# Weight sums rebuilt inside SBUF: a copy of the high parts and an accumulating transfer of the low parts, instead of a round trip through device memory

## Chip, cores and metric

The kernel runs on one core of one Trainium2 chip. The metric is the device time of one execution in microseconds (us). Before the change it is 1271.15 us, the median of three runs (1270.35 to 1272.01). The engines are named as in the profile: PE (TensorE, matrix products), DVE (VectorE), ACT (ScalarE), POOL (GpSimd), SP (SyncE, which here only issues transfers).

## The reference

Two stages, all in float32. First a channel attention on q, k, v of shape 2 x 6016 x 256; then a SwiGLU block on the 12032 rows of its output, with weights of 256 x 1536, 256 x 1536 and 1536 x 256.

```python
qn = q / (norm(q, axis=1) + 1e-6);  kn = k / (norm(k, axis=1) + 1e-6)
s  = kn.transpose(0, 2, 1) @ qn / tau          # 256 x 256 for each batch
a  = softmax(s, axis=-1)
x  = (v @ a).reshape(12032, 256)
xn = x / sqrt(mean(x*x) + 1e-6) * rms_g
g, val = xn @ w_gate, xn @ w_val               # 12032 x 1536 each
out = (g * sigmoid(g) * val) @ w_out           # 12032 x 256
```

## The kernel before

Every float32 product of the second stage is made of three matmuls on rounded operands: a value is kept as a high part (rounded to the type fp32r) and a low part (the rest, rounded), and high x high, high x low and low x high are added. So each weight stands twice in SBUF: `w_hl[0]` holds the high parts, `w_hl[1]` the low parts, for 12 chunks f = 0 to 11 of 128 hidden channels each.

The rows of x go in blocks j of 3 or 4 tiles of 128 rows. A step (j, f) is chunk f of block j. Blocks 0 and 1 are computed plainly (`emit_hidden`: six matmuls for `pg`, six for `pv`, ACT makes the silu, DVE multiplies into `zh` and splits the result into gx, gy or gz by turns; two steps later the PE matmuls `po` use it). From block 2 on a step uses seven products instead of eight (`new_products`), and for these the kernel needs sums and differences of weight columns: `build_s` makes them for the pairs p = 0 to 5 of chunks (2p, 2p + 1).

The weights come in as 64-bit words. In the steps of block 0 they are loaded (`load_w`), decoded on DVE and ACT into a float32 tile `wx` (`decode_w`, lines 119 to 138; two such tiles take turns) and split (`split_w`, line 144). Beside them the loads `raw` of q and k of the second batch run, whose scores PE computes in the same steps.

`build_s(p, piece)` works in four pieces, which stand in the steps of blocks 0 and 1 as a table of steps counted from (1, 0) has it:

```python
at_step = [
    (-2, 0, 3, 4), (-1, 2, 5, 6), (4, 5, 6, 7), (6, 8, 9, 10), (7, 9, 10, 11), (10, 12, 13, 14),
]
```

Piece 0 fills a tile `t` (called `wk` in the profile) of 128 x 1024 floats, 512 KB, with the float32 weights of two chunks; piece 1 is four DVE operations on it (line 621); piece 2 rounds on ACT (line 624); piece 3 takes the rests on DVE (line 627: two into `s`, one into `w`). There are two buffers: even p use one, odd p the other, so piece 0 of pair p waits for piece 3 of pair p - 2. The table gives pair 2 one step between pieces 0 and 1; pairs 3, 4 and 5 have two.

Each engine does its instructions in the order in which they are written. SP issues transfers one after another too: an issue that waits holds all that follow. In SP's queue of block 1 stand the 16 small transfers of `emit_xT_move` (line 553), which bring a transposed block `xw` into place as `xnT`; block 2 needs them.

POOL, in blocks 0 and 1, does the small operations behind the row norms (`ss` at line 484, `rr` at line 488, which ACT waits for to write `xn` at line 500), the low parts `vt` of v (line 417), and for block 2 the differences `xp` (lines 574 and 579) and the low parts `xt` (line 593). It also issues the transfers of line 145.

Of the kernel before, what the change touches and what calls it, by code (L numbers as in the profile page):

```python
# [8 lines left out]
F32 = mybir.dt.float32  # L9
# [3 lines left out]
ALU = mybir.AluOpType  # L13
AX = mybir.AxisListType

P = 128
# [3 lines left out]
def kernel(  # L20
# [17 lines left out]
    nc = tc.nc  # L38
# [3 lines left out]
    KC = C // P  # L42
    NF = DFF // P
# [35 lines left out]
    w_hl = [const.tile([P, NF * WF + 8 * (1 - i)], F32R, name=f"w{i}") for i in range(2)]  # L79
    w_hl = [  # L80
        w[:, 4 * (1 - i):4 * (1 - i) + NF * WF].rearrange("p (f n) -> p f n", f=NF)
        for i, w in enumerate(w_hl)
    ]
# [5 lines left out]
    def f32(ap):  # L89
        return ap.bitcast(F32)  # L90
# [8 lines left out]
    wval = {}  # L99
# [38 lines left out]
            )  # L138
            wval[f] = x.bitcast(F32)

    dram = ctx.enter_context(tc.tile_pool(name="dram", bufs=1, space=bass.MemoryType.DRAM))
    kept = [dram.tile([P, KC * 2 * P], F32, name=f"kept_{f}") for f in range(NF)]

    def split_w(f, engine=nc.gpsimd):
        nc.gpsimd.dma_start(out=kept[f], in_=wval[f][:, :KC * 2 * P])
        nc.scalar.activation(out=w_hl[0][:, f, :], in_=wval[f], func=AF.Copy)
        engine.tensor_tensor(
            out=w_hl[1][:, f, :], in0=wval.pop(f), in1=f32(w_hl[0][:, f, :]), op=ALU.subtract,
        )
# [6 lines left out]
    for b, sizes in enumerate(([2] * 2 + [4] * 9 + [2] * 3 + [1], [CH] * 11 + [3])):  # L156
        t = 0
# [174 lines left out]
    t = 0  # L332
# [268 lines left out]
    def build_s(p, piece):  # L601
        f0, f1 = 2 * p, 2 * p + 1
        if piece == 0:
            tag = "so1" if p % 2 else "wk"
            s_tmp[p] = pool[tag].tile([P, 4, 2 * P], F32, tag=tag, name=f"wk_{p}")

        t = s_tmp[p]
        if piece > 1:
            hi, lo = ([x[:, p, :2], x[:, p, 2], w[:, f1, :2 * P]] for x, w in zip(s_hl, w_hl))
            src = (t[:, 2:4], t[:, 0], t[:, 1])  # L610
        if piece == 0:
            for i, f in enumerate((f0, f1)):
                nc.sync.dma_start(
                    out=t[:, 2 * i:2 * i + 2].rearrange("p i n -> p (i n)"), in_=kept[f]
                )
        elif piece == 1:
            for o, i0, i1, op in (
                (3, 2, 3, ALU.add), (2, 0, 2, ALU.subtract),
                (0, 3, 0, ALU.subtract), (1, 1, 0, ALU.subtract),
            ):  # L620
                nc.vector.tensor_tensor(out=t[:, o], in0=t[:, i0], in1=t[:, i1], op=op)  # L621
        elif piece == 2:
            for o, x in zip(hi, src):
                nc.scalar.activation(out=o, in_=x, func=AF.Copy)
        else:
            for o, x, y in zip(lo, src, hi):
                nc.vector.tensor_tensor(out=o, in0=x, in1=f32(y), op=ALU.subtract)
# [371 lines left out]
    with tc.manual_schedule():  # L999
# [30 lines left out]
        def stir(n, name):  # L1030
# [11 lines left out]
            4: lambda: load_w(0),  # L1042
            7: lambda: (load_w(1), decode_w(0)),
            8: lambda: split_w(0),
            10: lambda: load_v_rows(0),
            11: lambda: decode_w(1),
            12: lambda: split_w(1),
            13: lambda: load_w(2),
        }
        for i in range(nch):  # L1050
            n = chunks[0][i][1]
# [93 lines left out]
        for f in range(NF):  # L1145
            go = [lambda: None]
            if f + 3 < NF:
                go = [lambda f=f: decode_w(f + 3, 0), lambda f=f: decode_w(f + 3, 1)]
            if f + 2 < NF:
                go.append(lambda f=f: split_w(f + 2, nc.vector))  # L1150
            if f + 3 < NF:
                go.append(lambda f=f: decode_w(f + 3, 2))
            weights[0, f] = go
            n = 2 if f % 2 else 1

            def more(n=n):
                fill(n)
                for _ in range(n):
                    square()
                    add()  # L1160

            at(0, f, more)
            if f + 5 < NF:
                at(0, f, lambda f=f: load_w(f + 5))
# [30 lines left out]
        for i in (2, 3, 0, 1):  # L1195
            for p in range(NP):
                j, f = divmod(NF + at_step[p][i], NF)
                go = lambda p=p, i=i: build_s(p, i)
                if j == 1:
                    weights.setdefault((j, f), [lambda: None]).append(go)  # L1200
                else:
                    at(j, f, go)
# [238 lines left out]
```

## Time and profile before

| What | Value |
|---|---|
| Three runs | 1270.35, 1271.15, 1272.01 us |
| The profiled execution | 1274.14 us, of which its span is 1272.4 us |
| PE busy | 1250.7 us (98%) |
| DVE, ACT, POOL busy | 875.0, 868.5, 793.6 us (69%, 68%, 62%) |
| Mean granted clock of PE | 0.997 of full speed |
| Transfers on POOL's queue (12 of 256 KB, line 145) | 3.15 MB |

The span begins with the first instruction. Blocks 0 and 1 lie between about 73 and 200 us; from about 206 us on the steps of seven products repeat to the end. A matmul's busy time says little by itself, since matmuls are pipelined; where PE loses time is seen in what it waits for. DVE's share is a mean over stages: in blocks 0 and 1 it has the decoding of the weights and the pieces of `build_s` to do beside the steps.

### The profile page before, as it was taken

To read this page: it belongs to the slowest core of one execution; us is meant where nothing else is said; L and a number is where in the kernel's file an instruction comes from. 1 tells how busy PE (TensorE), PEld (TensorE's weight loads), DVE (VectorE), ACT (ScalarE), POOL (GpSimd) and SP (SyncE) were. 2 spreads that over 40 slices of the span, in tenths; PEclk is the share of its full clock that TensorE was granted. 3 is DMA by queue.
4 is the path that set the end of the run, shared out by engine and by line. 5 is a ranking of instruction groups with operands and counts; after the bars stand their busy time and mean duration, and the time that the engine had idled before them with its cause. 6 is when DMAs were issued, how large, how long until landed. Compare 5 with 4: busy or idle time off the path is not lost.

```text
span 1272.4 us, 25236 instructions
## 1 busy us (share of the span) xinstructions
PE 1250.7 (98%) x9245; PEld 1196.4 (94%) x9245; DVE 875.0 (69%) x1571; ACT 868.5 (68%) x1771; POOL 793.6 (62%) x637
## 2 busy tenths in 40 slices
PE   9998989999999999999999999999999999999998
PEld 8798989999999999999999999999999999999997
DVE  5788867558767657667767667767766766766764
ACT  5566647677776786776677677667677777777653
POOL 0221224575777777777677777777777777776742
PEclk9999989999999999999999999999999999999999
DMA  8979332020220220220220211211211211211110
GB/s 296 318 247 303 114 82 65 17 35 18 51 34 18 51 34 18 51 34 18 45 41 18 45 27 32 43 26 34 41 27 34 40 26 37 37 23 27 18 18 17
DMA packets 231004, 78.20 MB, mean 61 GB/s; under 512 B 191200, under 2 KB 220128, under 8 KB 230880
## 3 DMA queue, kind: packets, MB, share of 16 engines
q1 hardware_dynamic: 229024, 72.13, 24.0%
q0 software_dynamic: 960, 3.15, 0.6%
q8 instruction: 72, 1.18, 0.4%
q10 hardware_dynamic: 896, 1.31, 0.4%
q14 instruction: 52, 0.43, 0.1%
HBM read 49.55 MB, written 15.47 MB: 51 GB/s over the span
## 4 chain that ended last, share of the span: by engine, by line
PE 84%; DVE 5%; DMA 5%; issue 2%; ACT 2%; SPq 1%; POOL 1%; POOLq 0%; DVEq 0%; ACTq 0%
PE pu L764 43%; PE po L940 26%; PE pq L764 7%; PE px L459 5%; PE s L185 2%; DMA raw<-in_k_dram 2%; PE po L890 1%; DVE wk L621 1%; SPq L553 1%; DMA raw<-in_q_dram 1%; DVE acc L210 1%; DMA wraw<-in_moe_w_out_dram 1%; DMA wraw<-in_moe_w_gate_dram 0%; DMA kept<-wx 0%; ACT xn L475 0%
## 5 line engine op out<-in xcount | busy, mean ns | idle before, releaser
L764 PE MATMUL pu<-xt,w 128*128 128x256 f32 x2376 | 407.8, 280 | 0.5 <-DVE zv L793 0.3
L764 PE MATMUL pu<-xt,s 128*128 128x256 f32 x2376 | 367.8, 281 | 0.9 <-ACT t L800 0.8
L764 PEld LDWEIGHTS pu<-xt,w 128*128 128x128 f32 x2376 | 344.0, 188 | 14.0 <-DVE zg L793 1.0
L764 PEld LDWEIGHTS pu<-xt,s 128*128 128x128 f32 x2376 | 327.3, 188 | 14.0 <-ACT zg L827 1.2
L732 POOL TENSOR_TENSOR gy<-zg,gy 128x512 fp32r<-128x512 f32 x131 | 182.3, 1392 | 150.3 <-ACT gy L726 86.3
L732 POOL TENSOR_TENSOR gx<-zg,gx 128x512 fp32r<-128x512 f32 (+1 forms) x131 | 201.1, 1535 | 86.5 <-ACT gx L726 84.9
L805 ACT ACTIVATE t<-pu 128x512 f32<-128x512 f32 x264 | 158.2, 599 | 98.6 <-PE pu L764 80.6
L940 PE MATMUL po<-gx,w 128*128 128x256 f32 (+1 forms) x927 | 197.1, 330 | 0.0
L793 DVE TENSOR_TENSOR zv<-pu,t 128x512 f32<-128x512 f32 x132 | 90.6, 686 | 112.9 <-ACT zg L827 83.3
L812 DVE TENSOR_TENSOR zg<-zg,zv 128x768 f32<-128x768 f32 x132 | 154.0, 1167 | 14.4 <-ACT t L800 0.5
L800 ACT ACTIVATE t<-pu 128x256 f32<-128x256 f32 x264 | 100.7, 381 | 86.7 <-PE pu L764 85.1
L726 ACT ACTIVATE gx<-zg 128x512 fp32r<-128x512 f32 (+1 forms) x132 | 95.8, 726 | 74.7 <-DVE zg L821 35.5
L940 PEld LDWEIGHTS po<-gx,w 128*128 128x128 f32 x927 | 136.5, 188 | 6.3 <-ACT os L976 0.2
L718 DVE TENSOR_TENSOR zg<-zg 128x256 f32<-128x256 f32 x228 | 97.0, 425 | 65.6 <-POOL gx L732 59.8
L764 PE MATMUL pq<-xt,w 128*128 128x256 f32 x792 | 135.9, 280 | 0.0
L793 DVE TENSOR_TENSOR zg<-pu,t 128x512 f32<-128x512 f32 x132 | 89.9, 681 | 48.5 <-PE pu L764 27.3
L940 PE MATMUL po<-gy,w 128*128 128x512 f32 x414 | 118.1, 393 | 0.0
L821 DVE TENSOR_TENSOR zg<-pu,zg 128x256 f32<-128x256 f32 x132 | 55.9, 424 | 87.6 <-PE pu L764 85.9
L732 POOL TENSOR_TENSOR gz<-zg,gz 128x512 fp32r<-128x512 f32 x57 | 113.4, 1989 | 0.0
L764 PEld LDWEIGHTS pq<-xt,w 128*128 128x128 f32 x792 | 112.0, 189 | 0.0
L809 ACT ACTIVATE zg<-zg 128x768 f32<-128x768 f32 x132 | 110.4, 837 | 0.0
L185 PE MATMUL s<-raw 128*128 128x256 f32 x376 | 86.9, 385 | 5.4 <-DMA raw<-in_k_dram 3.9
(152 smaller groups left out, 2007.9 us busy)
## 6 DMA issues: line engine op xcount, KB each, us to landing
xnT<-xw SPq DMA_DIRECT2D x352, 32.0 KB, 1.9
v<-in_v_dram SPq DMA_DIRECT2D x84, 128.0 KB, 3.7
raw<-in_q_dram SPq DMA_DIRECT2D x20, 512.0 KB, 4.9
out_dram<-ob SPq DMA_DIRECT2D x80, 128.0 KB, 3.2
raw<-in_k_dram SPq DMA_DIRECT2D x19, 512.0 KB, 6.5
wraw<-in_moe_w_gate_dram SPq DMA_DIRECT2D x12, 256.0 KB, 6.4
wraw<-in_moe_w_val_dram SPq DMA_DIRECT2D x12, 256.0 KB, 6.8
wraw<-in_moe_w_out_dram SPq DMA_DIRECT2D x12, 256.0 KB, 6.5
```

What stands on the lines that cost most here:

```text
L185: nc.tensor.matmul(out=s_ps[b][:, c, :], lhsT=r[:, 1, t, c * P:(c + 1) * P], rhs=r[:, 0, t, :], start=(t0 + t == 0 and c == 0), stop=(t0 + ...
L459: nc.tensor.matmul(out=px[:, i, :], lhsT=w[:, c, i * P:(i + 1) * P], rhs=x[:, c, :], start=(i == 0 and c == 0 and m == 0), stop=(c == KC - ...
L718: nc.vector.tensor_tensor(out=z[:, o], in0=z[:, i0], in1=z[:, i1], op=ALU.subtract)
L726: nc.scalar.activation(out=gh, in_=hh, func=AF.Copy)
L732: engine.tensor_tensor(out=gl, in0=hh, in1=f32(gh), op=ALU.subtract)
L764: nc.tensor.matmul(out=out, lhsT=wm[wi], rhs=xm[xi], start=(start and q == 0), stop=(q == 2), skip_group_check=True,)
L793: nc.vector.tensor_tensor(out=z[:, 1:], in0=u, in1=t[:, :2], op=ALU.add)
L800: nc.scalar.activation(out=mt[:, 0], in_=mu[:, 1], func=AF.Copy)
L805: nc.scalar.activation(out=nt[:, 1:], in_=nu, func=AF.Copy)
L809: nc.scalar.activation(out=zg[:, 1:], in_=zg[:, 1:], func=AF.Silu)
L812: nc.vector.tensor_tensor(out=zg[:, 1:], in0=zg[:, 1:], in1=z, op=ALU.mult)
L940: nc.tensor.matmul(out=acc[b][:, o:o + g.shape[-1]], lhsT=w, rhs=g, start=first, stop=True, skip_group_check=True,)
```

## The change

The device-memory tiles `kept` and the 12 transfers that fill them are gone. Piece 0 reads the high and low parts that stand in SBUF: one transfer copies the high parts of both chunks into `t`, and a second, issued from POOL, adds the low parts to what is there. The copy goes out on SP, for pair 2 on POOL. In the changed file all lines behind the first hunk are four lower.

```diff
-    dram = ctx.enter_context(tc.tile_pool(name="dram", bufs=1, space=bass.MemoryType.DRAM))
-    kept = [dram.tile([P, KC * 2 * P], F32, name=f"kept_{f}") for f in range(NF)]
-
     def split_w(f, engine=nc.gpsimd):
-        nc.gpsimd.dma_start(out=kept[f], in_=wval[f][:, :KC * 2 * P])
         nc.scalar.activation(out=w_hl[0][:, f, :], in_=wval[f], func=AF.Copy)
...
         if piece == 0:
-            for i, f in enumerate((f0, f1)):
-                nc.sync.dma_start(
-                    out=t[:, 2 * i:2 * i + 2].rearrange("p i n -> p (i n)"), in_=kept[f]
-                )
+            whole = t.rearrange("p (f i) n -> p f (i n)", f=2)
+            wh, wl = (f32(w[:, f0:f0 + 2, :KC * 2 * P]) for w in w_hl)
+            (nc.gpsimd if p == 2 else nc.sync).dma_start(out=whole, in_=wh)
+            nc.gpsimd.dma_start(out=whole, in_=wl, accum_op=ALU.add)
```

PE, DVE and ACT have the same instructions in the same order as before. POOL and SP don't. POOL in block 1, before, from the row norms of pair 1's time to the differences for block 2:

```order
L488 TENSOR_TENSOR rr_0_1339<-ss_0_1335,mhalf 128x2
L484 TENSOR_SCALAR ss_1_1439<-ss_1_1439 128x2
L488 TENSOR_TENSOR rr_1_1443<-ss_1_1439,mhalf 128x2
L242 TENSOR_TENSOR nrm_1508<-nrm_1508,half 128x4
L417 TENSOR_TENSOR vt_3_0_1630<-vw_0_1589,vt_3_0_1629 128x512
L574 TENSOR_TENSOR xp_1712<-xnT_1486 128x2x256
```

The same place in the changed kernel (w_97 holds the high parts, w_98 the low ones; the `wk` tiles are those of pairs 1, 2, 3 and 4 in this order):

```order
L484 TENSOR_TENSOR rr_0_1313<-ss_0_1309,mhalf 128x2
L611 DMA wk_1327<-w_98 128x2x512
L480 TENSOR_SCALAR ss_1_1413<-ss_1_1413 128x2
L484 TENSOR_TENSOR rr_1_1417<-ss_1_1413,mhalf 128x2
L238 TENSOR_TENSOR nrm_1482<-nrm_1482,half 128x4
L610 DMA wk_1547<-w_97 128x2x512
L611 DMA wk_1547<-w_98 128x2x512
L413 TENSOR_TENSOR vt_3_0_1604<-vw_0_1563,vt_3_0_1603 128x512
L611 DMA wk_1630<-w_98 128x2x512
L611 DMA wk_1668<-w_98 128x2x512
L570 TENSOR_TENSOR xp_1686<-xnT_1460 128x2x256
```

The adding transfers of pairs 3 and 4 now stand in POOL's queue ahead of the differences `xp`, and each waits there for its copy to land. At the end of block 1 POOL had, before:

```order
L593 TENSOR_TENSOR xt_2_1711<-xp_1712,xt_2_1710 128x512 x2
L484 TENSOR_SCALAR ss_0_1873<-ss_0_1873 128x2
L488 TENSOR_TENSOR rr_0_1877<-ss_0_1873,mhalf 128x2
L484 TENSOR_SCALAR ss_1_1914<-ss_1_1914 128x2
L488 TENSOR_TENSOR rr_1_1918<-ss_1_1914,mhalf 128x2
```

And in the changed kernel (`wk` is that of pair 5):

```order
L589 TENSOR_TENSOR xt_2_1685<-xp_1686,xt_2_1684 128x512 x2
L611 DMA wk_1817<-w_98 128x2x512
L480 TENSOR_SCALAR ss_0_1847<-ss_0_1847 128x2
L484 TENSOR_TENSOR rr_0_1851<-ss_0_1847,mhalf 128x2
L480 TENSOR_SCALAR ss_1_1888<-ss_1_1888 128x2
L484 TENSOR_TENSOR rr_1_1892<-ss_1_1888,mhalf 128x2
```

The adding transfer of pair 5 stands ahead of the row norms that ACT waits for at the start of block 2. On SP, before, from the 16 small transfers of block 2 on (pairs 2, 3, 4, then 5):

```order
L553 DMA xnT_1486<-xw_1483 32x2x128 x16
L613 DMA wk_1573<-kept_106 128x512
L613 DMA wk_1573<-kept_107 128x512
L613 DMA wk_1656<-kept_108 128x512
L613 DMA wk_1656<-kept_109 128x512
L613 DMA wk_1694<-kept_110 128x512
L613 DMA wk_1694<-kept_111 128x512
L355 DMA v_1732<-in_v_dram 32x32x32 x4
L613 DMA wk_1843<-kept_112 128x512
L613 DMA wk_1843<-kept_113 128x512
```

And in the changed kernel:

```order
L549 DMA xnT_1460<-xw_1457 32x2x128 x16
L610 DMA wk_1630<-w_97 128x2x512
L610 DMA wk_1668<-w_97 128x2x512
L351 DMA v_1706<-in_v_dram 32x32x32 x4
L610 DMA wk_1817<-w_97 128x2x512
```

Pair 2 is no longer behind the 16 small transfers; pairs 3, 4 and 5 keep their places, with one transfer each.

## Rows read from the trace of the kernel before

**Rows 1.** Busy time by stretch: length, PE, PEld, DVE, ACT, POOL, PE clock, DMA share, GB/s.
```profile
100.00:143.00 43.00, 39.31 (x231) 36.77 (x230) 39.75 (x55) 25.65 (x42) 6.83 (x9) 1.00 0.75 235
175.00:206.00 31.00, 26.96 (x179) 26.55 (x180) 28.09 (x51) 20.06 (x50) 11.85 (x12) 0.89 0.32 85
```
**Rows 2.** Waits of PE between 60 and 206 us: total, times, longest.
```profile
PE po L890 <- DVE gz L732: 4.8, 2, 4.6
PE pxt L526 <- ACT xn L500: 2.1, 1, 2.1
PE s L185 <- DMA raw<-in_k_dram: 2.0, 2, 1.6
```
**Rows 3.** The chain of waits between 90 and 103 us: start, length, what.
```profile
91.52 5.27 DMA kept<-wx
...
101.30 0.39 SPq L105
...
102.24 8.32 DMA wraw<-in_moe_w_out_dram
```
**Rows 4.** Issues between 101.2 and 103.2 us: size, time to landing.
```profile
wraw<-in_moe_w_gate_dram SPq DMA_DIRECT2D x1, 256.0 KB, 7.8
```
**Rows 5.** Timeline of SP between 130 and 215 us: start, length, issue.
```profile
143.10 2.04 SPq L613 DMA_DIRECT2D wk<-kept  x4
...
161.78 10.35 SPq L553 DMA_DIRECT2D xnT<-xw  x16
172.30 12.47 SPq L613 DMA_DIRECT2D wk<-kept  x6
...
196.61 0.82 SPq L613 DMA_DIRECT2D wk<-kept  x2
```
**Rows 6.** Timeline of SP between 179 and 181 us.
```profile
179.81 0.80 SPq L613 DMA_DIRECT2D wk<-kept  x2
```
**Rows 7.** Landings of tile wk between 179.5 and 181 us.
```profile
DMA to landing us min/median/max: 2.6/2.7/2.8
```
**Rows 8.** Tile kept between 135.5 and 139 us: issue in ns, landing.
```profile
L145 POOL DMA_DIRECT2D kept<-wx x1: 562/562/562, 135.8 to 135.8; - x1
...
DMA to landing us min/median/max: 2.3/2.3/2.3
```
**Rows 9.** Timeline of DVE between 130 and 215 us, idle time before in brackets.
```profile
152.50 1.80 DVE L621 TENSOR_TENSOR wk<-wk 128x256 f32<-128x256 f32 x4
...
165.31 0.42 DVE L627 TENSOR_TENSOR w<-wk,w 128x256 fp32r<-128x256 f32 x1
...
175.73 1.80 DVE L621 TENSOR_TENSOR wk<-wk 128x256 f32<-128x256 f32 x4 [8.12 <-DMA wk<-kept]
...
179.32 0.42 DVE L627 TENSOR_TENSOR w<-wk,w 128x256 fp32r<-128x256 f32 x1
...
185.72 2.82 DVE L621 TENSOR_TENSOR wk<-wk 128x256 f32<-128x256 f32 x4
...
196.13 0.41 DVE L627 TENSOR_TENSOR w<-wk,w 128x256 fp32r<-128x256 f32 x1
...
200.00 1.80 DVE L621 TENSOR_TENSOR wk<-wk 128x256 f32<-128x256 f32 x4 [0.73 <-DMA wk<-kept]
```
**Rows 10.** Timeline of PE between 130 and 215 us.
```profile
178.05 1.86 PE L890 MATMUL po<-w,gz 128*128 128x256 f32 x7 [4.57 <-DVE gz L732]
...
182.27 1.82 PE L847 MATMUL pg<-xt,w 128*128 128x384 f32 x6
183.93 1.21 PE L847 MATMUL pv<-xt,w 128*128 128x384 f32 x6
...
202.60 0.62 PE L764 MATMUL pu<-xt,s 128*128 128x256 f32 x3 [0.76 <-ACT t L800]
```
**Rows 11.** Timeline of POOL between 130 and 215 us.
```profile
161.76 1.01 POOL L242 TENSOR_TENSOR nrm<-nrm,half 128x4 f32<-128x4 f32 x1 [3.39 <-DVE nrm L241]
...
196.64 0.45 POOL L484 TENSOR_SCALAR ss<-ss 128x2 f32<-128x2 f32 x1 [2.59 <-ACT xn L475]
```

## Prediction

> **What bounds the kernel now.** I read the busy time by stretch first. From 206 us on PE is back to back, and the change touches nothing there, so the time moves only by what reaches PE before that. The waits of PE in blocks 0 and 1 say where it can [rows 2]: 4.6 us at once for `gz`, 2.1 us for `xn`, twice for `raw` (1.6 and 0.4 us); 0.76 us more stand at the start of block 2, for `t` [rows 10]. The first of them is the largest and belongs to pair 2 of `build_s`. DVE stands idle for 8.12 us before 175.73 for `wk<-kept` [rows 9]. The buffer was free when piece 3 of pair 0 ended, at 165.31 + 0.42 = 165.73 [rows 9], but SP was then issuing the 16 small transfers, 10.35 us from 161.78, and came to pair 2 at 172.30 [rows 5]. PE, with some steps in hand, lost 4.57 us of it, and then worked for a while at half clock: six matmuls in 1.82 us at 182.27, the like six in 1.21 us at 183.93 [rows 10], a mean granted clock of 0.89 over that stretch [rows 1] (half speed is 1.2 GHz, full is 2.4). Last I looked at DVE from 175 to 206 us: busy 28.09 of 31 us [rows 1], so after pair 2 it is DVE, not PE, that has no time to give away.
>
> **What goes: the 12 transfers into `kept` (a).** POOL's issue time doesn't matter, it is busy for 6.83 of 43 us there [rows 1]. What matters is the room in the DMA engines: between 100 and 143 us they are 0.75 busy [rows 1]. The chain of waits runs through one of these transfers (5.27 us, until 96.79) and then through a weight load of 8.32 us, until 110.56 [rows 3], behind which DVE, ACT and so the 2.1 us wait of PE lie. In such a queue 256 KB take 0.7 us: the first of three loads issued one after another lands at 101.30 + 7.8 = 109.1, the third at 110.56 [rows 3, 4], 1.46 us for two. Two transfers into `kept` fall ahead of that load and two ahead of the `raw` load of the 1.6 us wait, so up to 1.4 us each. I take 1.5 us of the first wait (the 1.4, and a little for the wait on `kept` itself), 0.8 of the second, since PE will come to it 1.5 us sooner, and 0.2 of the 0.4. Sum: -2.5 us. Bounds: 0, if other loads only fill the gap, and -4.1, if all three waits go (2.1 + 1.6 + 0.4).
>
> **What comes: a copy and then an addition, one after the other (b).** Before, two 256 KB loads went out together; now the addition may only start when the copy has landed, and POOL holds the wait.
>
> The copy, 512 KB: the two loads of a pair on quiet engines are issued from 179.81, the second 0.42 later, and land 2.6 to 2.8 us after each issue [rows 6, 7], the pair 3.2 us after the first. One transfer of 256 KB out of SBUF by POOL landed in 2.3 [rows 8]; another 0.7 for the second half gives 3.0. I take 3.1 (2.7 to 3.4).
>
> The addition, 512 KB: no row shows one. It must fetch both addends, so I count 3.1 and another 512 KB at 0.7 for 256 KB: 4.5 us. Lower bound 3.1, as if it were a plain copy; upper bound 6.2, as if it were two transfers in a row. I stay near the lower one because the two fetches can overlap.
> The Trainium skill has a price (Collectives: The Full Stack, The bandwidth ceiling: the fold count and why AG ≠ RS ≠ AR): an addition in the DMA engines is slower because it needs two source reads, not because of the adding. With the 2.0 us plus size by 436 GB/s of DMA: Bandwidth & Descriptors (Anatomy of one DMA) this would be an estimate of 2.0 + 2 x 1.2 = 4.4 us; no run here shows it yet, and the sum by it would be 0.2 to 0.3 us lower than mine.
>
> Now the chain, in the clock of the trace before:
>
> - Pair 0 and pair 1 are in time. Copy at 143.10 [rows 5], 143.1 + 3.1 + 4.5 = 150.7, needed at 152.50 [rows 9]; a margin of 1.8, which the `v` loads beside it may eat. Pair 1 is needed later.
> - Pair 2: POOL is done with `nrm` at 162.77 [rows 11], so the copy goes at 165.8, lands at 168.9, the sum at 173.4. DVE starts 2.3 us before the 175.73 of now, and PE's wait shrinks to about 2.2 us.
> The Trainium skill (DMA: Bandwidth & Descriptors, Issuing engines are not separate DMA queues) has it that starting transfers on several engines only saves issue time, usually small beside the transfer. By that rule the move of pair 2 to POOL would be worth nothing; the row differs in size, 10.35 us of issue [rows 5].
> - Pair 3 takes that back. Its buffer is free when piece 3 of pair 1 ends, 4.0 us after the start at 175.73 (179.74) [rows 9], so now at 177.4. Copy and addition: landed at 185.1. DVE, at its pace of now (10.0 us from 175.73 to 185.72), would be there at 183.4; it waits some 2 us. In the trace before it began at 185.72 without waiting, so 0.6 us of the 2.3 are left. Whether PE runs at half clock meanwhile no longer matters, as DVE waits anyway.
> - From there to the end of piece 3 of pair 3 DVE needs what it needs now, 185.72 to 196.54, 10.8 us [rows 9]. There is slowing by POOL in it: the four operations of 185.72 take 2.82 us, at 175.73 they took 1.80. This stays, because `xp` and `xt`, now behind the additions of pairs 3 and 4 in POOL's queue, fall into the same stretch. End: 195.9. Pair 4's sum is there in time (its copy can start at about 180).
> - Pair 5: copy at 196.0, landed at 199.1, and POOL, which waits for it and issues the addition (0.7 us, a little over the 0.56 that an issue of half the size took [rows 8]), comes to `ss` at 199.8 instead of 196.64 [rows 11]: 3.2 us later. Behind `ss` on POOL is `rr`; ACT waits for that to write `xn`, and behind `xn` in ACT's queue are the copies `t` that PE waits for at 202.60 [rows 10]. Nothing in that chain has slack: PE already waits 0.76 us there. DVE's side is no better: the sum of pair 5 lands at 203.6, and DVE waited for it until 200.00 [rows 9], with the first `zg` of block 2 close behind.
>
> So (b) costs +3.3 us at the start of block 2. Bounds: the copy enters it three times (pairs 2, 3, 5), the addition twice on POOL's side and three times on DVE's. With 2.7 and 3.1 it is 3.3 - 1.2 - 2.8 = -0.7; with 3.4 and 6.2, by DVE's side, 203.6 + 0.9 + 5.1 = 209.6 against 200.00, it is +9.6.
>
> **The clock at the start of block 2 (c).** PE has little to do there until `t` comes: its idle time grows from 0.76 to some 4 us. The row of 178.05 shows what 4.57 us idle did: half clock after it. In block 2 PE is the bound, so this costs up to what six matmuls lost (1.82 against 1.21) over a few us: 2 us, between 0 and 2.8. It fell for the like idle time, so I count it.
>
> **Sum.** -2.5 + 3.3 + 2.0 = +2.8 us on the profiled execution of 1274.14 us, which lies 3.0 above the median; taken from the median, 1271.15 + 2.8 = 1274.0 us. Within 0.2% (2.5 us) a measurement of this kernel can't be told from no change, so this is slower by a hair.
>
> **Rivals.**
>
> - *The gap doesn't pull the clock down, the rest as above*: -2.5 + 3.3 = +0.8, 1272.0 us, no change. For it: PE's 2.1 us wait at 113 us brought no fall [rows 1, 2]; the idle time now comes in pieces with matmuls between. Against: the pieces add up to about the 4.57 us that did.
> - *The additions run nearly like plain copies* (the other side): copy 2.9, addition 3.1. Then pair 3 lands with DVE (b is 3.3 - 0.6 - 2.8 = -0.1), PE's gap stays near 1 us and c is 0, and if (a) is 3 us the sum is -3.1: 1268 us. It decides when copy and addition together stay under about 6.2 us. For it: 512 KB is little beside the fixed part of a landing (2.3 us for 256 KB). Against: two fetches, and POOL must issue it.
> - *The addition costs two transfers, 6.2 us*: pair 0 comes at 152.4 and has no margin left, pair 5 lands at 203.6 + 5.1 = 208.7, b is +8.7 and c 2, with a at -2.5: 1279.3 us.
>
> **Chances.** Forecast 0.33, the dear addition 0.11: slower 0.44. No fall of the clock, or errors that cancel: 0.30 for no change. Cheap additions, or more from (a): 0.26 for faster. The forecast's own range is 1272.5 to 1276.5. The range for 8 in 10 takes in both other cases: 1267 (a at -3.5, b at -0.7) to 1280.
>
> **What would show it.** DVE's wait before the operations of pair 2 falls from 8.1 to about 6 us, and new waits of about 2 and 4 us appear before those of pairs 3 and 5, with the adding transfer as what ended them. POOL's `ss` at the end of block 1 starts after the copy of pair 5 has landed. PE reaches 143 us some 2.5 us earlier against the trace before, and the start of block 2 a little later, with the granted clock at 0.5 behind it. I am wrong if additions land in 3 us or less (then faster), if the waits of PE before 125 us stay (then slower still), or if DVE meets no wait at pair 3.

## The result and the profile after

The changed kernel takes 1284.07 us (median of four runs, 1283.39 to 1285.84); the kernel before, beside it, 1270.75 us. The ratio is 1.0107, with a 95% interval of 1.0089 to 1.0124: slower by 13.3 us. The prediction said slower by 2.8 us, 1274.0 us, with 1267 to 1280 as its range; the direction held, the size did not, and the time lies above the range. The profiled execution took 1283.53 us (span 1281.8), 9.4 us more than the profiled one of before, which lay 3.4 us over its median. Below, "us" for a kernel tried is its ratio to the kernel before times 1271, since each was timed beside runs of that kernel; a single such figure is sure to about 2 us.

Busy time by stretch, as in [rows 1] (length, PE, PEld, DVE, ACT, POOL, PE clock, DMA share, GB/s), first two stretches of before that [rows 1] doesn't have, then the changed kernel:

```profile
140.00:175.00 35.00, 32.89 (x216) 32.06 (x215) 20.67 (x39) 18.80 (x44) 6.49 (x7) 1.00 0.31 86
206.00:240.00 34.00, 33.97 (x247) 31.68 (x246) 17.53 (x31) 24.10 (x55) 23.45 (x21) 1.00 0.15 30
```

```profile
100.00:143.00 43.00, 43.00 (x260) 41.03 (x259) 39.75 (x56) 29.16 (x50) 5.17 (x4) 1.00 0.73 210
140.00:175.00 35.00, 30.03 (x182) 29.50 (x180) 18.23 (x36) 15.78 (x40) 11.54 (x11) 0.90 0.46 111
175.00:206.00 31.00, 22.94 (x139) 22.33 (x139) 20.49 (x37) 13.46 (x31) 13.13 (x13) 0.89 0.47 103
206.00:240.00 34.00, 31.45 (x216) 30.01 (x217) 18.53 (x36) 25.02 (x58) 18.66 (x19) 0.90 0.28 59
```

Between 100 and 143 us PE is never idle, where 3.7 us were lost before. How much of that the removal gave can't be read from these two profiles, for such waits differ from one execution to the next: of the kernels tried below, the one that keeps the 12 transfers (w1) lost 1.8 us there, and those without them 0 to 1.4; the runs of the removal alone (e1) tell. Then the later stretches lose: DVE falls from 28.09 to 20.49 busy us between 175 and 206, and PE's mean granted clock is 0.90 from 140 to 175 and from 206 to 240 us too, where it had been full before. A mean of 0.90 over 35 us is 7 us at 1.2 GHz. The waits of PE that count, each with the idle time ahead of it (timeline of PE, 150 to 215 us):

```profile
151.79 1.33 PE L886 MATMUL po<-w,gx 128*128 128x256 f32 x9 [1.98 <-ACT ob L910]
...
176.36 1.23 PE L886 MATMUL po<-w,gz 128*128 128x256 f32 x7 [4.35 <-DVE gz L728]
...
193.97 1.67 PE L886 MATMUL po<-w,gz 128*128 128x256 f32 x7 [4.94 <-DVE gz L728]
...
208.55 1.01 PE L760 MATMUL pu<-xt,w 128*128 128x256 f32 x3 [4.27 <-ACT t L801]
```

Before there was only one wait of more than 2.1 us [rows 2, 10]; now there are three of over 4 us, and a new one of 2 us at 151.79. At each of the four the clock fell, where before it fell once. Where DVE comes late is seen in its timeline (140 to 216 us), to be laid beside [rows 9]:

```profile
143.57 2.49 DVE L206 TENSOR_TENSOR acc<-acc,ob 128x1024 f32<-128x1024 f32 x1 [1.64 <-ACT ob L200]
...
147.96 1.80 DVE L617 TENSOR_TENSOR wk<-wk 128x256 f32<-128x256 f32 x4
...
174.03 1.80 DVE L617 TENSOR_TENSOR wk<-wk 128x256 f32<-128x256 f32 x4 [7.86 <-DMA wk<-w]
...
189.44 4.01 DVE L617 TENSOR_TENSOR wk<-wk 128x256 f32<-128x256 f32 x4 [6.27 <-DMA wk<-w]
...
194.30 2.81 DVE L617 TENSOR_TENSOR wk<-wk 128x256 f32<-128x256 f32 x4
...
199.99 0.41 DVE L623 TENSOR_TENSOR w<-wk,w 128x256 fp32r<-128x256 f32 x1
...
209.14 1.80 DVE L617 TENSOR_TENSOR wk<-wk 128x256 f32<-128x256 f32 x4 [6.01 <-DMA wk<-w]
```

The waits for pairs 2, 3 and 5 are 7.9, 6.3 and 6.0 us, where 6, 2 and 4 were expected. The operations of pair 4 are shorter than before (194.30); in the timeline of before, which [rows 9] shows without this line, they were:

```profile
189.95 4.39 DVE L621 TENSOR_TENSOR wk<-wk 128x256 f32<-128x256 f32 x4
```

POOL's timeline over the same time shows where the adding transfers (line 611) stand in its queue:

```profile
142.24 1.39 POOL L611 DMA_DIRECT2D wk<-w  x1 [11.16 <-PE pv L843]
143.22 1.75 POOL L413 TENSOR_TENSOR vt<-vw,vt 128x512 fp32r<-128x512 f32 x1
...
181.84 1.22 POOL L611 DMA_DIRECT2D wk<-w  x1 [10.36 <-DMA wk<-w]
185.08 1.19 POOL L611 DMA_DIRECT2D wk<-w  x1 [2.02 <-ACT xt L587]
...
204.10 1.20 POOL L611 DMA_DIRECT2D wk<-w  x1 [5.85 <-DMA wk<-w]
205.38 0.22 POOL L480 TENSOR_SCALAR ss<-ss 128x2 f32<-128x2 f32 x1
```

And the landings, from the view of tile `wk`, in this order: the copy of pair 5 (issued at 200.47), the addition of pair 5 (204.10), the addition of pair 3 (181.84):

```profile
DMA to landing us min/median/max: 3.1/3.1/3.1
...
DMA to landing us min/median/max: 5.0/5.0/5.0
...
DMA to landing us min/median/max: 7.6/7.6/7.6
```

The copy of pair 5 took what was expected, a lone addition half a us more, and the addition of pair 3 three us more.

### The profile page after: what moved, and what is told of

It is laid out like the page before. It is cut to its first block, busy times and chain, and to the rows that moved or that the text cites. A ratio compares the mean times of both kernels' runs of the same rounds, so it can differ in the third digit from the quotient of the medians.

```text
span 1281.8 us, 25208 instructions
## 1 busy us (share of the span) xinstructions
PE 1256.8 (98%) x9245; PEld 1203.0 (94%) x9245; DVE 872.4 (68%) x1571; ACT 871.0 (68%) x1771; POOL 796.3 (62%) x632
## 4 chain that ended last, share of the span: by engine, by line
PE 89%; DVE 3%; DMA 3%; issue 2%; ACT 2%; POOL 1%; ACTq 0%; SPq 0%; DVEq 0%; POOLq 0%
PE pu L760 43%; PE po L936 25%; PE pq L760 7%; PE px L455 5%; PE s L181 4%; DMA raw<-in_k_dram 2%; PE po L886 2%; DMA wk<-w 1%; PE pg L843 1%; PE pv L843 1%; DVE wk L617 1%; DVE acc L206 0%; ACT xn L471 0%; DVE zh L857 0%; DVE gx L728 0%
```

## The experiments

**What the two good halves are worth.** First the removal by itself, then the copies without additions.

```diff
# e1_no_writes, against the kernel before
-        nc.gpsimd.dma_start(out=kept[f], in_=wval[f][:, :KC * 2 * P])
...
-                    out=t[:, 2 * i:2 * i + 2].rearrange("p i n -> p (i n)"), in_=kept[f]
+                    out=t[:, 2 * i:2 * i + 2], in_=qr[0][:, 2 * f:2 * f + 2]
# e2_copy_only, against the changed kernel
-            nc.gpsimd.dma_start(out=whole, in_=wl, accum_op=ALU.add)
```

> The kernel before, without the 12 transfers into kept; the loads of build_s read rows of q of the same size in their place, so the values of the sums are others. Theory A (what I predicted, term a): the removal alone makes the kernel 2.5 us faster, 1268.3 us, bounds 0 and 4.1 us. Theory B (the removal also sets off the fall of the clock at 153 us that the changed kernel shows): PE comes to 143 us about 4.5 us sooner, waits some 2 us for ob at 151 us and falls to half clock for about 7 us; of the 4.5 us some 3 are given back, and the time is within 1.5 us of the kernel before, 1269 to 1272 us.

> The changed kernel without its six adding transfers: the copies of the high parts alone, so the low parts are left out of the sums. Theory A (the additions and the waits for them are what costs): without them the delay at the start of block 2 goes, and the time is about that of the removal alone, 1267 to 1270 us; no wait of DVE for wk before the operations of pairs 3 and 5, and only one or two falls of the clock. Theory B (the falls of the clock come from PE's new phase and not from the additions): three or more falls stay, and at least 6 of the 13.3 us stay, 1277 us or more.

Measured: the removal 1267.84 us, ratio 0.9973 (0.9961 to 0.9986), -3.4 us: theory A. The copies alone 1263.78 us, 0.9944 (0.9928 to 0.9960), -7.1 us, with no fall of the clock before the last microseconds; it beat even theory A. DVE's wait for pair 2 tells the two apart (timeline of DVE, the removal first):

```profile
172.77 1.80 DVE L617 TENSOR_TENSOR wk<-wk 128x256 f32<-128x256 f32 x4 [8.20 <-DMA wk<-in_q_dram]
```

```profile
164.69 1.80 DVE L616 TENSOR_TENSOR wk<-wk 128x256 f32<-128x256 f32 x4 [2.35 <-DMA wk<-w]
```

So the change had two gains in it: 3.4 us from the transfers removed, and 3.7 us from the copies. In the profiles the second one lies at pair 2, which is no longer on SP's queue: from its first operation for pair 0 to that for pair 2 DVE takes 17.5 us with the copies and 23.3 with the removal alone. The six additions cost 20.7 us (1.0107 - 0.9944).

**Is it the adding?** The second transfer as a plain copy:

```diff
# e3_plain_second, against the changed kernel
-            nc.gpsimd.dma_start(out=whole, in_=wl, accum_op=ALU.add)
+            nc.gpsimd.dma_start(out=whole, in_=wl)
```

> The changed kernel with the second transfer a plain copy of the low parts over the high parts, not an addition; same queues, same waits, same bytes in. It leaves the high parts out of the sums. Theory A (two transfers in a row are dear in themselves, whatever the second does): the second lands about 3.5 us after its issue in place of 5.0, and the time falls by less than half of the 13.3 us, 1279 us or more. Theory B (the addition is dear: 5.0 us alone, 7.6 to 8.1 beside another): with plain copies the pair takes some 7 us in place of 8.6 to 12, and more than half of the 13.3 us goes, 1272 to 1276 us.

Measured: 1282.05 us, 1.0084 (1.0067 to 1.0102). Only 2.9 of the 20.7 us go (the interval overlaps with that of the changed kernel, so even these are not sure): theory A. Second transfers of pairs 5 and 3, tile `wk`:

```profile
DMA to landing us min/median/max: 3.4/3.4/3.4
...
DMA to landing us min/median/max: 7.7/7.7/7.7
```

Alone it lands 1.6 us sooner than an addition; at pair 3, beside other transfers, no sooner. So a second transfer in a row, behind a wait in POOL's queue, is dear in itself, whether it adds or not.

**Which pairs.** The additions of some pairs alone, each against the changed kernel:

```diff
+            if p < 2:          # e6_add_p0_p1;  e7_add_p2_to_p4: 1 < p < 5;  e8_add_p5: p == 5
                 nc.gpsimd.dma_start(out=whole, in_=wl, accum_op=ALU.add)
# likewise e9_add_p3: p == 3;  e12_add_p1: p == 1
```

> The changed kernel with the adding transfer for pairs 0 and 1 only; the low parts of pairs 2 to 5 are left out. Theory A (the new fall of the clock at 153 us comes from the first addition: its issue of 1.4 us on POOL pushes vt beside DVE's 128x1024 operation, which takes 2.5 us in place of 1.2, ob is 1.2 us late and PE waits 2 us): the wait for ob of some 2 us and the fall at 153 us are there, and the time is 3 to 5 us above the copies alone, 1267 to 1269 us. Theory B (pairs 0 and 1 are in time and cost nothing, as I predicted): 1263 to 1265 us and no fall of the clock before 170 us.

> The changed kernel with the adding transfer for pairs 2, 3 and 4 only; the low parts of pairs 0, 1 and 5 are left out. Theory A (each addition on the path adds its 5 us and more, and the falls of the clock come on top): DVE waits for pair 2 about 5 us and for pair 3 about 6 us, two falls of the clock, 8 to 12 us above the copies alone, 1272 to 1276 us. Theory B (most is lost at pairs 0, 1 and 5): at most 5 us, 1269 us or less.

> The changed kernel with the adding transfer for pair 5 only; the low parts of pairs 0 to 4 are left out. Theory A (as I predicted in terms b and c, but by the measured 3.1 us of the copy and 1.2 us of issue: ss some 4 us late, then PE at half clock): 4 to 6 us above the copies alone, 1268 to 1270 us, with a fall of the clock at the start of block 2. Theory B (the additions of the pairs before had only used up all slack, and pair 5 alone meets some): 2 us or less, 1266 us or less.

Measured: 1266.88 us, 0.9966 (0.9952 to 0.9980); 1275.12 us, 1.0031 (1.0021 to 1.0040); 1270.06 us, 0.9989 (0.9978 to 0.9999). Over the copies alone that is 2.8, 11.1 and 5.7 us, theory A each time (pairs 0 and 1 a little under its 3 to 5 us), and they add up to 19.6 of the 20.7: within the noise the additions act one by one. DVE in the kernel with pairs 2 to 4 waits for pair 3 as theory A had it, but for pair 2 8.1 us, where 5 was expected:

```profile
147.01 1.80 DVE L618 TENSOR_TENSOR wk<-wk 128x256 f32<-128x256 f32 x4
...
170.17 1.80 DVE L618 TENSOR_TENSOR wk<-wk 128x256 f32<-128x256 f32 x4 [8.06 <-DMA wk<-w]
...
185.51 4.09 DVE L618 TENSOR_TENSOR wk<-wk 128x256 f32<-128x256 f32 x4 [6.24 <-DMA wk<-w]
```

**Pairs 0 and 1.** Their sums land before DVE gets to them, so why 2.8 us? I first gave pair 0 to POOL, then left pair 1 alone.

```diff
# e10_p0_by_pool, against the changed kernel (pair 1 keeps copy and addition)
+            if p == 0:
+                nc.gpsimd.tensor_tensor(out=whole, in0=wh, in1=wl, op=ALU.add)
...
```

> As the kernel with additions for pairs 0 and 1 only, but the sum of pair 0 is one operation of POOL (128x1024, about 2.7 us) before its vt, in place of copy and adding transfer; pair 1 keeps copy and addition, the low parts of pairs 2 to 5 are left out. Theory A (the 3.1 us of pairs 0 and 1 come from pair 0's addition, whose issue pushes vt beside DVE's 128x1024 operation): that operation takes 1.2 us again, the wait for ob is under 1.5 us, no fall of the clock at 153 us, 1263.5 to 1265 us. Theory B (pair 1's addition is enough for it): the wait for ob stays at 2 us and the clock falls, 1266 to 1268 us.

> The changed kernel with the adding transfer for pair 1 only; the low parts of the other pairs are left out. Theory A (of the 3.1 us of pairs 0 and 1 pair 0's addition makes all, since its issue pushes vt beside DVE's 128x1024 operation): that operation takes 1.2 us, the wait for ob is 1.5 us or less, no fall of the clock at 153 us longer than 3.4 us, 1263 to 1265 us. Theory B (pair 1's issue of 1.3 us on POOL is enough): the wait for ob is 2 us, the clock falls for 6.8 us, 1266 to 1268 us.

e10: 1267.3 us, 0.9970 (0.9959 to 0.9981), wait for `ob` 2.2 us and the clock fell, as theory B has it. But it doesn't tell: DVE's operation was at 1.22 us again, as A wanted, while ACT was late elsewhere (a new 0.67 us wait of PE for `z`); POOL's 2.7 us at 130 us, which e10 brought in, are the likely reason. e12 is the clean one: 1264.18 us, 0.9943 (0.9929 to 0.9958), nothing over the copies alone: theory A. From pair 0 to pair 2 DVE takes 20.8 us in e6 and 17.5 in e12, as with the copies alone. The operation before `ob`, with both additions (e6) and with pair 1's alone (e12), timelines of POOL and of DVE:

```profile
142.06 1.40 POOL L612 DMA_DIRECT2D wk<-w  x1 [12.23 <-DVE gz L729]
143.04 1.75 POOL L413 TENSOR_TENSOR vt<-vw,vt 128x512 fp32r<-128x512 f32 x1
...
143.30 2.58 DVE L206 TENSOR_TENSOR acc<-acc,ob 128x1024 f32<-128x1024 f32 x1 [1.63 <-ACT ob L200]
```

```profile
143.87 1.30 POOL L413 TENSOR_TENSOR vt<-vw,vt 128x512 fp32r<-128x512 f32 x1 [11.84 <-DVE gz L729]
...
145.50 1.22 DVE L206 TENSOR_TENSOR acc<-acc,ob 128x1024 f32<-128x1024 f32 x1 [1.63 <-ACT ob L200]
```

And the stretch from 140 to 175 us of the same two:

```profile
140.00:175.00 35.00, 32.68 (x204) 32.37 (x203) 22.96 (x45) 19.69 (x47) 11.95 (x12) 0.90 0.39 104
```

```profile
140.00:175.00 35.00, 33.66 (x231) 33.24 (x230) 24.96 (x48) 21.67 (x51) 11.78 (x12) 1.00 0.38 107
```

And PE's wait for `ob`, in e6 and then with the copies alone:

```profile
151.61 1.33 PE L887 MATMUL po<-w,gx 128*128 128x256 f32 x9 [2.32 <-ACT ob L911]
```

```profile
151.07 1.33 PE L885 MATMUL po<-w,gx 128*128 128x256 f32 x9 [0.82 <-ACT ob L909]
```

Pair 0's addition, issued at 142.06, holds POOL for a microsecond; `vt` slides behind it from DVE's idle 1.6 us into DVE's 128x1024 operation, which takes 1.4 us longer; the `zh` behind that on DVE, ACT's `gx` (idle for 3.25 in place of 1.90 us) and `ob` are late by as much, PE waits 2.3 us, against 0.8 with the copies alone and 1.3 in e12, and the clock falls.

**Pair 3**, whose addition took 7.6 us:

> The changed kernel with the adding transfer for pair 3 only; the low parts of the other pairs are left out. In the changed kernel it took 7.6 us to land, beside the addition of pair 4, that pair's copy and four loads of v. Theory A (the other addition slows it): alone it lands in 5 to 5.5 us, and costs 2 to 4 us over the copies alone, 1266 to 1268 us. Theory B (the loads of v and the copy beside it are enough): it lands in 6.5 us or more, and costs 4 us or more, 1268 to 1270 us.

Measured: 1268.58 us, 0.9975 (0.9964 to 0.9986), 3.9 us over the copies alone; the addition landed 7.7 us after its issue with no other addition in flight. On the landing theory B is right, the price lies at the border. The landing (tile `wk`) and the stretch in which it was in flight:

```profile
DMA to landing us min/median/max: 7.7/7.7/7.7
```

```profile
175.20:182.90 7.70, 6.06 (x40) 5.86 (x39) 0.42 (x2) 2.25 (x5) 7.16 (x7) 1.00 0.99 193
```

Pair 4's copy and four loads of `v` were in flight beside it, and the share of the DMA engines is 0.99. It is added up from the times of packets and can pass 1 (1.14 in the changed kernel from 181.8 to 189.4 us), so it shows engines at work throughout, but not that no room was left. The profile of this run also has a short fall of the clock before 175 us, which pair 3 can't have made, so part of the 3.9 us may not be its own. Which of the copy and the loads weighs more was not tried, and pairs 2 and 4, which make up the other 7 us of the 11.1, were not taken apart.

**Pair 5.** Its addition moved behind `ss` and `rr` on POOL, and, apart from that, PE kept busy through its wait.

```diff
# e11_p5_behind, against e8_add_p5: the adding transfer as a piece of its own
...
+                if i == 4:
+                    if p == 5:
+                        at(2, 0, lambda: build_s(5, 4))
...
# e13_p5_busy, against e8_add_p5: before the step (2, 1)
+                        b = ps_gv.tile([P, 512], F32, tag="q", bufs=1, name="busy")
+                        for _ in range(24):
+                            nc.tensor.matmul(
+                                out=b[:, :384], lhsT=w_hl[0][:, 0, :P], rhs=w_hl[0][:, 0, P:4 * P],
+                                start=True, stop=True,
+                            )
```

> As the kernel with the addition for pair 5 only, but its adding transfer stands on POOL behind the two ss and rr of the end of block 1; the low parts of pairs 0 to 4 are left out. Theory A (POOL's queue is what costs: ss goes 5 us late because the addition ahead of it waits for the copy): ss is at its old place, PE's wait for t of 4.3 us falls under 1.5 us, no fall of the clock, 1264 to 1266 us. Theory B (DVE's wait for the same sum is as long, 6 us, and holds zg and the buffers of pu): PE waits 3 us or more a little later, the clock falls, 1268 to 1270 us.

> As the kernel with the addition for pair 5 only, and with 24 matmuls of 128x384 that nobody reads put into PE's order just before the matmuls that waited 4.3 us there; the low parts of pairs 0 to 4 are left out. Theory A (3.4 us of the 6.3 us that pair 5 costs are the half clock of 6.8 us behind PE's wait): PE is busy through the wait, the clock stays full at the start of block 2, and the time falls by 2.5 to 3.5 us, to 1266.5 to 1267.5 us. Theory B (the wait alone makes the 6.3 us, PE's slowness then is hidden by DVE, which is late itself): the time stays within 1 us of 1270.1 us, or rises by the matmuls that don't fit into the gap.

e11: 1269.77 us, 0.9990 (0.9981 to 1.0000), no gain: theory B. `ss` ran at its old place, but PE met a wait of the same size a little later, for DVE. PE with the addition in place, and then moved:

```profile
194.39 1.01 PE L761 MATMUL pu<-xt,w 128*128 128x256 f32 x3 [4.28 <-ACT t L802]
```

```profile
200.23 1.01 PE L765 MATMUL pu<-xt,w 128*128 128x256 f32 x3 [4.42 <-DVE zg L794]
```

POOL's queue and DVE's own wait for the sum cost the same, and either is enough. e13: 1268.90 us, 0.9981 (0.9970 to 0.9992), 1.0 us less than e8, between the theories and nearer to B. The two intervals overlap; that there is a difference rests on the profiles below. The clock stayed full:

```profile
192.06 4.37 PE L1398 MATMUL busy<-w 128*128 128x384 f32 x24
196.50 0.62 PE L761 MATMUL pu<-xt,w 128*128 128x256 f32 x3
```

From the last `po` of block 1 to the first `po` of block 2 it is 18.0 us here (191.13 to 209.16), 19.0 in e8 (189.02 to 208.01) and 13.5 with the copies alone (188.87 to 202.34): of 5.5 us lost there the half clock makes 1.0, the wait itself 4.5. The slow time costs less than it looks: the clock was down from 192.1 us, 2.3 us before PE had work again, and e13 keeps a wait of 0.84 us for the next `t` that e8 doesn't have.

**Other ways to the sum.** One operation of POOL or of DVE in place of both transfers:

```diff
# e4_pool_add; e5_dve_add has nc.vector
-            (nc.gpsimd if p == 2 else nc.sync).dma_start(out=whole, in_=wh)
-            nc.gpsimd.dma_start(out=whole, in_=wl, accum_op=ALU.add)
+            nc.gpsimd.tensor_tensor(out=whole, in0=wh, in1=wl, op=ALU.add)
```

> The changed kernel with each pair's copy and addition replaced by one addition of POOL over 128x1024 into the same tile, no transfer at all. From POOL's 1.32 us for 128x512 I expect 2.6 us for each, alone. Theory A (latency of the two transfers is what costs): 2.6 us in place of 8.6 to 12 takes DVE's waits for wk below 2 us each and the start of block 2 back; 1266 to 1270 us, faster than both kernels. Theory B (POOL's queue and its slowing of DVE decide): POOL, which has xp, xt and ss to do in 175 to 206 us, comes late to them and slows the operations of DVE beside it; 1271 to 1276 us.

> The changed kernel with each pair's copy and addition replaced by one addition of VectorE over 128x1024 into the same tile, no transfer and nothing on POOL. Six operations of about 1.2 us (the 128x1024 row of DVE), 7.2 us more of DVE. Theory A (waiting for the transfers is what cost; DVE's own time is dearer than POOL's in block 1, where it was busy 28 of 31 us from 175 to 206 us): pairs 2 to 5 add some 4 us to a DVE that is late there already, no wait for wk: 1265 to 1269 us. Theory B (DVE is the bound in all of block 1, so every us of it shows): the copies-alone time 1263.8 + 7.2 = 1271 us or more, with at least one fall of the clock.

e4: 1275.7 us, 1.0035 (1.0021 to 1.0048), theory B. It has no wait for a transfer, but POOL's operation takes 2.6 us, and DVE's four for pair 3, beside POOL, take 4.7, where the kernel before had 2.8 [rows 9] (timelines of POOL and of DVE):

```profile
180.35 2.56 POOL L610 TENSOR_TENSOR wk<-w,w 128x1024 f32<-128x1024 f32 x1 [1.39 <-DVE w L622]
```

```profile
181.70 4.69 DVE L616 TENSOR_TENSOR wk<-wk 128x256 f32<-128x256 f32 x4
```

e5: 1271.15 us, 0.9995 (0.9986 to 1.0005), theory B: its six operations of 1.23 us are 7.4 us, and 6.5 us show. In both PE waited 2.4 us for `ob` and the clock fell behind it.

**The version that beats both.** The kernel before, with only the two loads of pair 2 put on POOL's queue:

```diff
# w1_p2_pool, against the kernel before
-                nc.sync.dma_start(
+                (nc.gpsimd if p == 2 else nc.sync).dma_start(
...
```

> The kernel before with only the two loads of pair 2 moved from SP's queue to POOL's, ahead of vt there; kept and all else as before. Theory A (the 8.1 us wait of DVE and the fall of the clock behind it come from SP issuing 16 transfers first): both go, as in the copies alone against the removal alone, 4 us: 1266 to 1268 us. Theory B (another wait takes its place, or POOL's issue of the two delays vt): 1269 us or more.

Measured: 1266.58 us, 0.9963 (0.9948 to 0.9977), -4.7 us: theory A. Timeline of DVE, then the stretch of [rows 1]:

```profile
168.00 1.80 DVE L621 TENSOR_TENSOR wk<-wk 128x256 f32<-128x256 f32 x4 [2.82 <-DMA wk<-kept]
```

```profile
175.00:206.00 31.00, 28.64 (x209) 27.12 (x208) 27.44 (x49) 21.49 (x53) 12.38 (x13) 1.00 0.32 79
```

The 8.12 us of [rows 9] are 2.8, and the clock no longer falls. From pair 0 to pair 2 DVE takes 17.9 us, 23.2 before.

## Why the prediction was right in direction and wrong in size

The yardstick is DVE's way from the first operation of pair 0 to that of pair 5, since the prediction was worked out in its clock: 47.5 us before, 51.1 by the prediction, 61.2 measured. The 10.1 us between the last two are about what the time was off by; the points below share them out.

- **The removal (a), -2.5:** right. The removal alone measured -3.4, within the bounds of 0 to -4.1, and PE lost nothing from 100 to 143 us in its profile.
- **Copy, 3.1:** right on quiet engines (3.07 to 3.17 for pairs 3 and 5); 3.6 to 3.8 for pairs 2 and 4, 4.3 and 4.8 for pairs 0 and 1, which ran beside loads of `v` and each other.
- **"Pair 0 and pair 1 are in time":** the first error. For pair 0 the landing came before its use (147.42 us, used at 147.96), but by luck: the sum landed 10.1 us after the copy's issue, where 7.6 had been predicted, and a DVE that nothing held would have been there after 9.2 to 9.4 us (e2, e7, e8, e9). The margin of 1.8 us was gone, and it only looked kept because DVE was late itself. What made DVE late is what I had left out, POOL's own queue: the issue took 1.39 us, not 0.7, and moved `vt` beside a DVE operation. I had followed only what waits for the sum, not what stands behind its issue. That this alone brings the wait for `ob` and the fall of the clock is seen in e3: there the sum landed after 8.4 us, in time, and PE still waited 2.2 us; how much the late landing would add by itself no run shows. Pair 0 to pair 2 on DVE took 26.1 us after the change, 23.2 without these two additions (e7): 2.9 us of the 10.1. The fall of the clock at 153 us, which the prediction didn't have, lies in this stretch.
- **Pair 2, 2.3 us earlier:** it came no earlier. With 23.2 us (e7) against 23.2 before, the gain of leaving SP's queue was just eaten: measured in e7 from the issue of pair 0's copy, the copy of pair 2 went out 0.3 later than predicted, took 0.5 more, the addition was issued 0.3 later and took 0.9 more. That is 2.0 of the 2.3 us, another share of the 10.1. The wait of PE there, forecast at 2.2 us, stayed at 4.4.
- **The addition, 4.5 us (b):** the step that failed most. Alone 5.0 us, close; at pair 3 7.6, above the upper bound of 6.2 (and 8.1 at pair 4, beside it). I priced it on quiet engines, though pair 4's copy and the loads of `v` stand right behind it in SP's queue. Pair 2 to pair 3 took 15.4 us, 11.7 by the prediction, 3.7 of the 10.1: 3.1 from the longer landing, 0.6 from the time between the copy's landing and the issue of the addition, which the prediction set at nothing. The 0.6 us that pair 3 was to keep of pair 2's gain, and the whole claim that pairs 2 to 4 would cost about nothing against before, go with it.
- **Pair 5:** mechanism right, on POOL and on DVE as said. From pair 3 to pair 5 19.7 us against 18.5, 1.2 of the 10.1: 0.5 from the time between the copy's landing (203.54) and the issue of the addition (204.10), 0.5 from the addition, 0.2 from DVE's work between. That work took 11.0 us, near the 10.8 kept from before, but only by luck: the four operations of pair 3 took 1.2 us more (4.01 against 2.82) and those of pair 4 1.6 us less (2.81 against 4.39). By itself the pair cost 5.7 us; (b) and (c) said 5.3, with 0.6 us of gain from pair 2 in it. `ss` stood 5.0 us late, not 3.2 (e8 against e2: 191.23 and 186.19). The +3.3 of (b) is 3.2 by the prediction's own figures (199.8 against 196.64).
- **The clock (c), 2.0:** that fall came, and cost 1.0 us at this place (e13), not 2.0. But it was one of four: of the others the prediction had only the one behind pair 2, and held that it no longer mattered. The 1.82 us from which it sized the term are not those of half clock either, since the clock rose within them (mean 0.64 from 182.27 to 184.09 us); the changed kernel's six matmuls at half clock took 2.27 us (154.24).
- **The rival of the dear addition, 1279.3,** was the nearest, with 6.2 us for every addition; it too had no price for POOL's issue at pair 0 nor for the transfers beside pair 3.

The estimate for the addition worked out from the Trainium skill, 4.4 us (Collectives: The Full Stack, The bandwidth ceiling: the fold count and why AG ≠ RS ≠ AR), was near the 5.0 measured alone and far from the 7.6. The Trainium skill's rule on several engines that start transfers (DMA: Bandwidth & Descriptors, Issuing engines are not separate DMA queues) lets such a move save issue time only, usually little beside the transfer. Issue time is what the move of pair 2 saved, but here it was not little: SP spent 10.35 us on 16 other transfers first [rows 5], and the move was worth 4.7 us (w1). The prediction's reading, that by the rule it would be worth nothing, went too far.

## What to carry to other kernels

A transfer that must wait for another one costs more than its landing: it blocks the in-order queue of the engine that issues it, so list what stands behind the issue as well as who waits for the data, also where the data seem to come in time. Price a landing by what else is in flight at that moment, not by the quietest row. And take a change of several parts apart: here two parts gained 7 us together, and a third one lost three times that.

## Not expected of the hardware

- The packets of an accumulating transfer took the DMA engines well over twice as long as those of a plain one of the same 512 KB: a share of 0.62 over the 5.0 us from 204.1 (3.1 us of all engines) against 0.41 over the 3.3 us of the plain second transfer of e3 (1.35 us); the two stretches stand below. Its issue took POOL 1.2 to 1.4 us, the plain one of e3 0.72 to 0.92.
- DVE's 128x1024 addition took 2.5 us beside POOL's 128x512 operation and 1.22 without it.
- The clock and the wait for `ob` at 151 us: after waits of 2.0 to 2.4 us (the changed kernel, e3, e4, e5, e6, e10) it fell every time; after 0.6 to 1.3 us in seven others (the kernel before among them) it didn't; with 1.4 us it fell in e9 and not in e13, and in e11 it fell with 1.0 us, in both for 3.4 us in place of 6.8. What decides between these stays open.

The stretches of the first point (the DMA share is the last value but one), the changed kernel and then e3:

```profile
204.10:209.10 5.00, 0.73 (x4) 0.55 (x3) 0.00 (x0) 2.06 (x7) 3.06 (x5) 0.88 0.62 107
```

```profile
204.70:208.00 3.30, 0.40 (x4) 0.19 (x2) 0.00 (x0) 1.49 (x7) 1.62 (x3) 1.00 0.41 161
```
